# A recurrence feeding a gated FFN on one core: shorter weight conversion, the diagonal term on TensorE, smaller loads, a first batch in three units, scores copied whole

## The chip, the cores and the metric

The kernel runs on one core of one Trainium2 chip. The metric is the device time of one execution in microseconds (us); smaller is better. The engines of the core are TensorE (PE, with PEld for its weight loads), VectorE (DVE), ScalarE (ACT), GpSimd (POOL) and SyncE (SP), which here issues every transfer. Each engine has its own queue and takes its instructions in order.

## The reference

A recurrence over time in 4 batches, 8 heads, 768 tokens, head dimension 48, and an FFN on its result:

```python
for t in range(S):
    cur = np.einsum('bhd,bhe->bhde', u[None] * k[:, :, t], v[:, :, t])
    y[:, :, t] = np.einsum('bhd,bhde->bhe', r[:, :, t], state + cur)
    state = w[None, :, :, None] * state + np.einsum('bhd,bhe->bhde', k[:, :, t], v[:, :, t])
x = y.transpose(0, 2, 1, 3).reshape(B, S, H * D)           # 4 x 768 x 384
h = np.maximum(x @ w_in, 0.0)                              # 384 -> 1024
conv[t] = conv_w[0] * h[t-1] + conv_w[1] * h[t] + conv_w[2] * h[t+1]
out = (h * sigmoid(conv)) @ w_out                          # 1024 -> 384
```

The three FFN weights arrive as float64; the rest is float32.

## The kernel before

**The recurrence** is computed in chunks of 64 tokens; two chunks make a group of 128 tokens, six groups a batch, 24 groups in all. Heads go in pairs, A on partitions 64 to 111 and B on 0 to 47. For a group g:

- `load(g)` brings k and r with the head dimension on partitions (KR, 448 KB), k and r with tokens on partitions (KRT, 384 KB) and v (WW, 384 KB, half of it zeros).
- `prep(g)` scales KR by powers of the decay (TKR), copies the scaled r into the images RA and RB, makes the products of r, k and u on KRT and sums them over the head dimension (L450, into QQ): this is the diagonal term, a token's own r·u·k. POOL writes QQ into the diagonal of the score rows of RA and RB (affine_select, L462) and scaled k goes into KTA and KTB.
- `scores(g)` multiplies k and r on PE into psC (L477, L478), and DVE copies what lies under the mask into RA and RB (copy_predicated, L481, 64 partitions each).
- `step(g, c)` makes, for each chunk, the new state on PE (L493, L494, "S" below), which ACT copies from psS back to WW, and the chunk's outputs (L507, L508, "av" below) into psY.
- `yout(g)` copies psY to YY, moves the last head pair into place by six small transfers, and splits the result into a high part and a low part in XT.

**The FFN** works on units of about half a batch, each in 8 blocks of 128 hidden features. `first(i)` makes 9 products (L569) into one of two PSUM tiles HP, then relu, the middle tap, two more taps (CV, L577), sigmoid, the gate product SG (L581) and the split into GH and GL. `second(i)`, three blocks later, makes 9 products into PO (L598). Each matrix product of the FFN is made of three, so as to keep float32 accuracy: high by high, high by low, low by high.

**Weights** come in 17 pieces through `convert`: one of ACT and three of DVE (L398, L400, L402) make float32 out of the float64 bit pattern, ACT makes the high part and DVE or POOL subtracts for the low part.

**Order.** All this is first recorded as operations with durations and data keys; a list scheduler (`Plan`) puts them in one fixed order for each engine, by its own costs and by the offsets in `OFF`. Operations marked "any" go to DVE or POOL, whichever the planner thinks is free (their line is that of the helper `tt`, L288; transfers have that of `dma`, L291). The planner also places products with zeros (L653) where PE would rest. The program asks for as many thirds of groups (`pieces`) as the next FFN unit needs: `need(0)` is 4 groups for the first unit of 382 tokens.

Of the kernel before, what the change touches and what calls it, by code (L numbers as in the profile page):

```python
# [27 lines left out]
OFF = {  # microseconds by which classes of operations come earlier  # L28
# [26 lines left out]
U = 386                 # most tokens of a unit of the FFN  # L55
PAT = {"2": [(0, 382), (382, 386)], "s": [(0, 384), (384, 384)]}  # units of a batch: first token, tokens
UNITS = [(b,) + x for b in range(B) for x in PAT[UP[b]]]
NU = len(UNITS)
WS = 256.0              # the weights on chip are scaled by this


class Plan:
    """Operations in a valid order, with the resources they take and the data they read and write. They are
    issued in the order of a list schedule: each engine takes, of what can start, what the tensor engine's
    sequence needs first."""
# [3 lines left out]
    def __init__(self):  # L69
        self.ops = []  # L70
        self.last_w, self.last_r = {}, {}

    def op(self, eng, dur, rd, wr, fn, cls="", x=0.0):
# [19 lines left out]
        self.ops.append((dur, x, sorted(pred), fn, cls))  # L93
        return n
# [18 lines left out]
    def order(self):  # L113
# [22 lines left out]
        while todo:  # L136
# [30 lines left out]
            if e == "pe":  # L167
                # zero products where the engine would rest and its clock with it
# [19 lines left out]
                if att and cls not in ATT:  # L188
                    free[e] += 0.065
# [8 lines left out]
                # the part of the block before the end of the tick  # L198
# [13 lines left out]
            elif e == "sp":  # L212
                free[e] = s + d + 0.04
                dq = max(dq, s + d + 0.65) + x
# [3 lines left out]
            else:  # L218
                free[e] = s + d
# [17 lines left out]
LAT, LPE = 0.15, 0.21  # L237
ATT = ("th", "sc", "S", "av")


def rwkv_ffn_kernel(tc, krd, krt, vt, wd, ut, w_in, conv_w, w_out, out):
# [4 lines left out]
    with ExitStack() as ctx:  # L246
# [14 lines left out]
        KRT = sb([128, 2, NP, 2, D], F32, "KRT", NBUF)  # L261
# [22 lines left out]
        def tt(eng, n, rd, wr, cls="", **kw):  # L284
# [3 lines left out]
            op(eng, d, rd, wr, lambda e: e.tensor_tensor(**kw), cls)  # L288
# [18 lines left out]
        dma([], ["wc"], wc, wd)  # L307

# [14 lines left out]
        dma([], ["uu"], uu, ut)  # L323
# [3 lines left out]
        for o in (0, 64):  # L327
# [16 lines left out]
        # powers of the decay: PW[j] = w^j, TK = w^(31-j), TR = w^(j-32), DN = w^(95-j)  # L344
# [19 lines left out]
        op("dve", 0.53, ["PW"], ["PW2"], powers2)  # L364
        op("act", 0.32, ["PW", "PW2"], ["DN"], lambda e: A.copy(DN, PW[:, :, 95:31:-1]))
# [22 lines left out]
        ncv = [0]  # L388

        def convert(src, n, dst, view, keys):  # L390
# [5 lines left out]
            op("act", act(n), [("ST", i)], [("CC", i)],  # L396
               lambda e: A.activation(cc, s2[:, :, 1].bitcast(F32), AF.Copy, scale=2.0 ** -111))
            op("dve", dve(n, 1.6), [("ST", i)], [("TT", i)], lambda e: V.tensor_scalar(  # L398
                out=t, in0=s2[:, :, 1], scalar1=-2 ** 31, scalar2=None, op0=ALU.bitwise_and))
            op("dve", dve(n), [("CC", i)], [("TT", i)], lambda e: V.scalar_tensor_tensor(  # L400
                out=t, in0=cc.bitcast(I32), scalar=3, in1=t, op0=ALU.logical_shift_left, op1=ALU.bitwise_or))
            op("dve", dve(n), [("ST", i)], [("TT", i)], lambda e: V.scalar_tensor_tensor(  # L402
                out=t, in0=s2[:, :, 0], scalar=29, in1=t, op0=ALU.logical_shift_right, op1=ALU.bitwise_or))
# [19 lines left out]
        def prep(g):  # L423
            i = g % NBUF
            k_t, r_t = KRT[i][:, 0], KRT[i][:, 1]
# [16 lines left out]
            if g < DR:
                for o, T, nm in ((64, RA, "a"), (0, RB, "b")):
                    tt("dve", 512, ["TR1", "TR2", ("KR", i)], [("Rr", i, nm)] + ([("Rz", i)] if o == 0 else []),
                       out=v2(T[i], o, o + 48), in0=v2(RR[i], o, o + 48), in1=c2(TR[o:o + 48], 48), op=ALU.mult)
            else:
                for o, T, nm in ((64, RA, "a"), (0, RB, "b")):
                    dma([("KR", i)], [("Rr", i, nm)] + ([("Rz", i)] if o == 0 else []), T[i][o:o + 48], RR[i][o:o + 48], 0.625, 0.27, "rmv")
            tt("any", 384, [], [("KRT", i)], cls="p", out=r_t, in0=r_t, in1=k_t, op=ALU.mult)
            op("dve", dve(384), [("KRT", i)], [("QQ", i)], lambda e: V.tensor_reduce(  # L450
                out=QQ[i], in_=r_t.rearrange("q p c d -> q (p c) d"), op=ALU.add, axis=AX.X))
# [16 lines left out]
        def scores(g):  # L468
            i = g % NBUF
            ra, rb = (RA[i], RB[i]) if g < DR else (RR[i], RR[i])  # L470

            def mm(e):
                for c in range(2):
                    for p in range(NP):
                        t = slice(c * C, (c + 1) * C)
                        n = (2 * p + c) * C
                        PE.matmul(psC[0:64, n:n + C], KK[i][64:112, p, t], ra[64:112, p, t], start=True, stop=True)  # L477
                        PE.matmul(psC[64:128, n:n + C], KK[i][0:48, p, t], rb[0:48, p, t], start=True, stop=True)  # L478
            op("pe", 1.263, [("KR", i)] + ([("Rr", i, "a"), ("Rr", i, "b")] if g < DR else []), ["psAs", "psBs"], mm, "sc", 768)
            for o, T, ps, nm in ((0, RA, psC, "a"), (64, RB, psC, "b")):  # L480
                op("dve", 0.62, ["psAs" if o == 0 else "psBs", "mask"], [("Rs", i, nm)], lambda e, o=o, T=T, ps=ps: V.copy_predicated(  # L481
# [4 lines left out]
        def step(g, c):  # L486
            i = g % NBUF
            b, gi = divmod(g, GPB)
            if not (gi == GPB - 1 and c == 1):
                def smm(e):  # L490
                    for p in range(NP):
# [4 lines left out]
                op("pe", 0.495, [("KTk", i, "a"), ("KTk", i, "b"), ("KTd", i, "a", c), ("KTd", i, "b", c), ("KTd", i), ("Wv", i),  # L496
                                ("WS", i, c)], ["psAu", "psBu"], smm, "S", 720)
# [11 lines left out]
            op("pe", 0.6, [("Wv", i), ("WS", i, c), ("Rr", i, "a"), ("Rr", i, "b"), ("Rs", i, "a"), ("Rs", i, "b"), ("Rz", i)],  # L509
# [43 lines left out]
        def first(i):  # L553
# [18 lines left out]
            op("pe", 9 * (n + 8) / 2400.0, [("wi", 0, f), ("wi", 1, f), ("X", b % 2, 0), ("X", b % 2, S + 1)] + xs, [H_], mm, "f1", 9 * n)  # L572
# [15 lines left out]
        def second(i):  # L588
# [4 lines left out]
            for m in range(NM):  # L593
# [6 lines left out]
                op("pe", 3 * (n + 8) / 2400.0, [("wo", 0, f), ("wo", 1, f), ("GH", gi), ("GL", gi)], [f"o{m}"], mm, "f2", 3 * n)  # L600
# [116 lines left out]
```

## Time and profile before

| what | value |
|---|---|
| runs | 344.4, 344.5, 347.0 us (median 344.5) |
| span of the profiled execution | 343.2 us |
| busy PE, PEld, DVE, ACT, POOL | 311.8, 285.1, 270.4, 206.5, 193.7 us |
| first product of the FFN starts | 50.5 us |
| bytes read, written | 36.3 MB, 4.7 MB |
| mean granted clock of PE, 0 to 50.5, 50.5 to 124.5, then | 0.80, 0.91, 1.00 |

A busy share is an average over the span, and stages differ. An engine's busy time in a stretch says what holds that stretch; the idle time in front of an instruction, with what ended it, says what was late. A product's recorded length holds its way through the array, so the rate of PE is read from the distance of starts, not from lengths.

### The profile page before, as it was taken

The page shows a single profiled execution, that of the slowest core. Times are in us where ns is not written, and L with a number is a line of the kernel's source. Part 1 is how long each engine was busy: PE and PEld are TensorE (multiplying, and loading weights), DVE is VectorE, ACT ScalarE, POOL GpSimd, SP SyncE. Part 2 cuts the span into 40 slices and gives each one's busy share as a digit, 9 for nine tenths or more (in the row PEclk, how much of TensorE's full clock was granted, in tenths as well). Part 3 has the DMA queues.
Part 4 walks back from the last instruction along what each step waited for, and adds up shares of the span by engine and source line. Part 5 has one row for each costly group of instructions (what it writes and reads, how often), then busy time and mean ns, then how long its engine had stood idle before and what let it go on. Part 6 is the DMA issues. An engine that isn't in the chain of part 4 may idle for free.

```text
span 343.2 us, 8886 instructions
## 1 busy us (share of the span) xinstructions
PE 311.8 (91%) x3487; PEld 285.1 (83%) x3487; DVE 270.4 (79%) x409; ACT 206.5 (60%) x468; POOL 193.7 (56%) x200
## 2 busy tenths in 40 slices
PE   8698694997779988999998999899999999999996
PEld 4486474896668988899997999898999999999995
DVE  6899989989999999978778786786775756565550
ACT  4343446584765765567575663685566755876752
POOL 5998998697899988727455463333231212243230
PEclk9768969698998999999999999999999999999999
DMA  7996975977864297365566571544530200200101
GB/s 192 328 261 166 289 216 173 304 181 218 262 196 124 55 313 214 97 201 165 149 181 174 147 217 50 145 141 135 157 96 13 72 1 2 77 5 1 71 0 70
DMA packets 23882, 50.25 MB, mean 146 GB/s; under 512 B 4448, under 2 KB 10848, under 8 KB 23840
## 3 DMA queue, kind: packets, MB, share of 16 engines
q1 hardware_dynamic: 23840, 49.69, 50.0%
q8 instruction: 27, 0.44, 0.6%
q14 instruction: 15, 0.12, 0.1%
HBM read 36.30 MB, written 4.72 MB: 120 GB/s over the span
## 4 chain that ended last, share of the span: by engine, by line
PE 53%; DVE 17%; POOL 8%; issue 7%; DMA 7%; ACT 6%; SPq 1%; DVEq 0%; POOLq 0%; ACTq 0%
PE HP L569 20%; PE PO L598 19%; DMA KR<-in_krd_dram 4%; PE psC L477 4%; PE psY L507 3%; DVE CV L577 3%; PE psS L493 3%; POOL KRT L288 2%; DVE KR L288 2%; ACT SG L580 2%; DVE RB L481 2%; POOL RA L462 1%; DVE KRT L288 1%; DVE RA L481 1%; PE PO L653 1%
## 5 line engine op out<-in xcount | busy, mean ns | idle before, releaser
L569 PE MATMUL HP<-XT,wi 128*128 128x386 f32 (+2 forms) x576 | 116.1, 347 | 5.0 <-DVE SG L581 5.0
L598 PE MATMUL PO<-GH,wo 128*128 128x384 f32 (+2 forms) x384 | 111.6, 345 | 4.1 <-POOL wo L288 3.3
L569 PEld LDWEIGHTS HP<-XT,wi 128*128 128x128 f32 x576 | 103.4, 192 | 8.5 <-DVE SG L581 4.9
L288 POOL TENSOR_TENSOR GL<-SG,GH 128x384 fp32r<-128x384 f32 (+2 forms) x50 | 53.5, 1070 | 97.5 <-ACT GH L583 87.1
L577 DVE SCALAR_TENSOR_TENSOR CV<-HP,cw,CV 128x384 f32<-128x384 f32 (+2 forms) x128 | 78.2, 614 | 25.4 <-ACT CV L574 23.5
L598 PEld LDWEIGHTS PO<-GH,wo 128*128 128x128 f32 x384 | 71.0, 189 | 6.5 <-POOL wo L288 3.9
L598 PE MATMUL PO<-GL,wo 128*128 128x384 f32 (+2 forms) x192 | 65.3, 340 | 0.0
L580 ACT ACTIVATE SG<-CV 128x384 f32<-128x384 f32 (+2 forms) x64 | 33.5, 524 | 45.8 <-DVE CV L577 45.4
L581 DVE TENSOR_TENSOR SG<-HP,SG 128x384 f32<-128x384 f32 (+2 forms) x64 | 35.5, 555 | 21.1 <-ACT SG L580 20.4
L573 ACT ACTIVATE HP<-HP 128x386 f32<-128x386 f32 (+2 forms) x64 | 30.5, 477 | 23.2 <-PE HP L569 22.5
L583 ACT CAST GH<-SG 128x384 fp32r<-128x384 f32 (+2 forms) x64 | 32.8, 512 | 13.7 <-DVE SG L581 13.7
L500 ACT COPY WW<-psS 48x192 f32<-48x192 f32 x88 | 27.3, 311 | 20.3 <-PE psS L494 15.6
L288 DVE TENSOR_TENSOR KR<-KR,TKR 112x1024 f32<-112x1024 f32 (+1 forms) x24 | 36.2, 1509 | 3.9 <-DMA KR<-in_krd_dram 3.9
L574 ACT ACTIVATE CV<-HP,cw 128x384 f32<-128x384 f32 (+2 forms) x64 | 37.1, 579 | 1.3
L493 PEld LDWEIGHTS psS<-WW,KTA 112*48 112x48 f32 x352 | 21.6, 136 | 18.5 <-ACT WW L500 9.4
L493 PE MATMUL psS<-WW,KTA 112*48 112x48 f32 x352 | 27.2, 224 | 10.3 <-ACT WW L500 7.3
L598 PEld LDWEIGHTS PO<-GL,wo 128*128 128x128 f32 x192 | 36.5, 190 | 0.0
L507 PE MATMUL psY<-RA,WW 112*48 112x64 f32 x384 | 32.9, 233 | 0.9 <-ACT WW L500 0.9
L508 PE MATMUL psY<-RB,WW 128*48 128x64 f32 x384 | 32.4, 233 | 0.3 <-DVE RB L481 0.3
L477 PE MATMUL psC<-KR 48*64 48x64 f32 x352 | 26.2, 227 | 5.0 <-DVE RB L481 3.8
L507 PEld LDWEIGHTS psY<-RA,WW 112*48 112x48 f32 x384 | 26.5, 133 | 4.0 <-issue 2.2
L477 PEld LDWEIGHTS psC<-KR 48*64 48x64 f32 x352 | 23.1, 140 | 7.2 <-DVE RB L481 4.0
(80 smaller groups left out, 505.4 us busy)
## 6 DMA issues: line engine op xcount, KB each, us to landing
KR<-in_krd_dram SPq DMA_DIRECT2D x24, 448.0 KB, 4.6
KRT<-in_krt_dram SPq DMA_DIRECT2D x24, 384.0 KB, 5.5
WW<-in_vt_dram SPq DMA_DIRECT2D x24, 384.0 KB, 5.0
out_dram<-OS SPq DMA_DIRECT2D x18, 192.0 KB, 2.0
ST<-in_w_in_dram SPq DMA_DIRECT2D x8, 384.0 KB, 5.8
ST<-in_w_out_dram SPq DMA_DIRECT2D x8, 384.0 KB, 4.5
RA<-KR SPq DMA_DIRECT2D x22, 96.0 KB, 4.5
RB<-KR SPq DMA_DIRECT2D x22, 96.0 KB, 4.1
```

Source lines behind the costliest of these rows:

```text
L288: op(eng, d, rd, wr, lambda e: e.tensor_tensor(**kw), cls)
L477: PE.matmul(psC[0:64, n:n + C], KK[i][64:112, p, t], ra[64:112, p, t], start=True, stop=True)
L493: PE.matmul(psS[64:112, n:n + D], KTA[i][:, p, c, :], WA[i][:, p, c, :], start=True, stop=True)
L507: PE.matmul(psY[64:112, n:n + C], WA[i][:, p, c, :], RA[i][0:112, p, t], start=True, stop=True)
L508: PE.matmul(psY[0:48, n:n + C], WB[i][:, p, c, :], RB[i][:, p, t], start=True, stop=True)
L569: PE.matmul(hp, wi[a][:, j, fs], X[:, x, j, t], start=(j == 0 and k == 0), stop=(j == 2 and k == 2))
L574: op("act", act(n) + 0.05, [H_, "cw"], [("T", ti)], lambda e: A.activation(t1, hp[:, 1:n + 1], AF.Copy, scale=cw[:, 3 * f + 1:3 * f + 2]), ...
L577: op("dve", dve(n + 60), [H_, "cw"], [("T", ti)], lambda e, k=k: V.scalar_tensor_tensor(out=t1, in0=hp[:, k:n + k], scalar=cw[:, 3 * f + k ...
L580: op("act", act(n), [("T", ti)], [("SG", ti)], lambda e: A.activation(sg, t1, AF.Sigmoid))
L581: op("dve", dve(n), [H_], [("SG", ti)], lambda e: V.tensor_tensor(out=sg, in0=hp[:, 1:n + 1], in1=sg, op=ALU.mult), "GG")
L583: op("act", act(n), [("SG", ti)], [("GH", gi)], lambda e: A.copy(gh, sg))
L598: PE.matmul(PO[m][:, :n], wo[a][:, f, ms], g2[x], start=(f == 0 and k == 0), stop=(f == NF - 1 and k == 2))
```

## The change

It does these things:

- `convert`: ACT's scaling becomes a Prelu whose slope for negative values carries the sign, so that the step at L402 goes; the remaining pair of DVE operations is one shift and one shift-and-or.
- The diagonal term: KP = KK·RR for a group (112x512, on DVE or POOL), then 16 products on PE of 64 rows by one column with u·w (`uw`) as the moving operand, into columns 192 to 199 of psS ("q" below), and a copy to QQ on ACT. The products on KRT and the reduction go.
- `scores`, from the third group on: a 128x512 image SC holds the diagonal (eye·QQ, on DVE or POOL), one copy_predicated of 128 partitions writes the masked scores over it, and two transfers of 128 KB move its halves into RA and RB. The two affine_selects on POOL stay in groups 0 and 1 alone.
- Loads: of KRT only k (KT, 192 KB), of WW only the two blocks that aren't zero (two of 96 KB); the zero rows are written by POOL, at the start and, for the state, at each batch's start. RA and RB of groups 0 and 1 are copied by ACT rather than multiplied by DVE.
- The first batch is 3 units of 254, 256 and 258 tokens, so 72 blocks in all and not 64, and `need(0)` is 2 groups.
- The planner's costs of S, av, scores, products, a switch between recurrence and FFN (`SWITCH`), a transfer, and of DVE beside POOL change, and with them the whole order.

The core of the diff:

```diff
-UP = '2sss'
+UP = '3sss'
-PAT = {"2": [(0, 382), (382, 386)], "s": [(0, 384), (384, 384)]}
+PAT = {"2": ..., "s": ..., "3": [(0, 254), (254, 256), (510, 258)]}
-LAT, LPE = 0.15, 0.21
-ATT = ("th", "sc", "S", "av")
+LAT, LPE = 0.18, 0.21
+SLOWER, SHARED, SWITCH, XFER = 0.8, 1.25, 0.19, 1.45
+ATT = ("th", "sc", "S", "av", "q")
...
-            dma([], [("KRT", i)], KRT[i], krt[g], 0.45, 1.1, "ldT")
-            dma([], [("Wv", i), ("WS", i, 0), ("WS", i, 1)], WW[i], vt[g], 0.45, 1.1, "ldV")
+            dma([], [("KT", i)], KT[i], krt[g, :, 0], 0.45, 0.55, "ldT")
+            dma([], [("Wv", i, "a")], WA[i][0:64], vt[g, 0:64, 0], 0.45, 0.27, "ldV")
+            dma([], [("Wv", i, "b")], WB[i][64:128], vt[g, 64:128, 1], 0.45, 0.27, "ldV")
...
-               lambda e: A.activation(cc, s2[:, :, 1].bitcast(F32), AF.Copy, scale=2.0 ** -111))
-            op("dve", dve(n, 1.6), [("ST", i)], [("TT", i)], lambda e: V.tensor_scalar(
-                out=t, in0=s2[:, :, 1], scalar1=-2 ** 31, scalar2=None, op0=ALU.bitwise_and))
+            op("act", act(n), [("ST", i)], [("CC", i)], lambda e: A.activation(
+                cc, s2[:, :, 1].bitcast(F32), AF.Prelu, scale=2.0 ** -111, alpha=2.0 ** 32))
+            op("dve", dve(n, 2), [("ST", i)], [("TT", i)], lambda e: V.tensor_scalar(
+                out=t, in0=s2[:, :, 0], scalar1=29, scalar2=None, op0=ALU.logical_shift_right), port=True)
-            op("dve", dve(n), [("ST", i)], [("TT", i)], lambda e: V.scalar_tensor_tensor(
-                out=t, in0=s2[:, :, 0], scalar=29, in1=t, op0=ALU.logical_shift_right, op1=ALU.bitwise_or))
...
-            tt("any", 384, [], [("KRT", i)], cls="p", out=r_t, in0=r_t, in1=k_t, op=ALU.mult)
-            op("dve", dve(384), [("KRT", i)], [("QQ", i)], lambda e: V.tensor_reduce(
-                out=QQ[i], in_=r_t.rearrange("q p c d -> q (p c) d"), op=ALU.add, axis=AX.X))
+            tt("any", 512, [("KK", i), ("RR", i)], [("KP", g % 2)], out=kp, in0=KK[i], in1=RR[i], op=ALU.mult)
+            def qmm(e):
+                for p in range(NP):
+                    for c in range(2):
+                        n, t = NP * D + 2 * p + c, slice(c * C, (c + 1) * C)
+                        PE.matmul(psS[0:64, n:n + 1], kp[64:112, p, t], uw[64:112, p:p + 1], start=True, stop=True)
+                        PE.matmul(psS[64:128, n:n + 1], kp[0:48, p, t], uw[0:48, p:p + 1], start=True, stop=True)
+            op("act", 0.2, ["psAu", "psBu"], [("QQ", i)], lambda e: A.copy(QQ[i], psS[:, NP * D:NP * D + 2 * NP]))
...
+            if g >= DS:
+                sc = SC[g % 2].rearrange("q (a t) -> q a t", t=C)
+                op("dve", 0.68, ["psAs", "psBs", "mask"], [("SC", g % 2)], lambda e: V.copy_predicated(
+                    out=sc, mask=mask.unsqueeze(1).broadcast_to([128, NP * 2, C]), data=psC.rearrange("q (a t) -> q a t", t=C)), "Rs")
+                for o, T, nm in ((0, RA, "a"), (64, RB, "b")):
+                    dma([("SC", g % 2)], [("Rs", i, nm)], T[i][o:o + 64].rearrange("q p t -> q (p t)"), SC[g % 2][o:o + 64], 0.5, 0.36, "smv")
+                return
```

How the order changes is seen at three places. DVE at the first block of the FFN (CC, TT and ST are the buffers of the weight conversion, CV the gate's taps). Before:

```order
L400 SCALAR_TENSOR_TENSOR TT_115<-CC_112,TT_115 128x384
L398 TENSOR_SCALAR TT_116<-ST_110 128x384
L402 SCALAR_TENSOR_TENSOR TT_115<-ST_109,TT_115 128x384
L400 SCALAR_TENSOR_TENSOR TT_116<-CC_113,TT_116 128x384
L481 COPY_PREDICATED RA_61<-mask,psC 64x512
L402 SCALAR_TENSOR_TENSOR TT_116<-ST_110,TT_116 128x384
L481 COPY_PREDICATED RB_64<-mask,psC 64x512
L577 SCALAR_TENSOR_TENSOR CV_89<-HP_120,cw,CV_89 128x382
```

After, at the same place:

```order
L518 COPY_PREDICATED SC_135<-mask,psC 128x512
L424 SCALAR_TENSOR_TENSOR TT_116<-CC_113,TT_116 128x384
L422 TENSOR_SCALAR TT_118<-ST_112 128x384
L424 SCALAR_TENSOR_TENSOR TT_118<-CC_115,TT_118 128x384
L298 TENSOR_TENSOR XT_89<-YY_87,XT_89 128x3x128
L298 TENSOR_TENSOR wi_141<-TT_116,wi_140 128x3x128
L298 TENSOR_TENSOR KR_69<-KR_69,TKR 112x1024
L298 TENSOR_TENSOR KP_83<-KR_69 112x512
L620 SCALAR_TENSOR_TENSOR CV_91<-HP_122,cw,CV_91 128x254
```

A piece of weights has two rows on DVE where it had three, and a group's scores one where they had two; the first CV is DVE's row 47 where it was row 75.

SP's queue (all transfers) after the first groups; RA and RB are the images that the outputs read, YY the small moves of finished outputs. Before:

```order
L291 DMA RA_61<-KR_67 48x512
L291 DMA RB_64<-KR_67 48x512
L291 DMA YY_86<-YY_86 16x256 x2
L291 DMA WW_78<-in_vt_dram 128x768
L291 DMA YY_86<-YY_86 16x256
L291 DMA KTA_70<-KRT_79 64x384
L291 DMA KTB_73<-KRT_79 64x384
L291 DMA KR_67<-in_krd_dram 112x1024
```

After:

```order
L301 DMA KR_68<-in_krd_dram 112x1024
L301 DMA KTB_75<-KT_81 64x384
L301 DMA WW_78<-in_vt_dram 64x384 x2
L301 DMA YY_87<-YY_87 16x256 x2
L301 DMA RA_62<-SC_135 64x512
L301 DMA RB_65<-SC_135 64x512
L301 DMA YY_87<-YY_87 16x256 x4
L301 DMA RA_63<-SC_134 64x512
L301 DMA RB_66<-SC_134 64x512
L301 DMA KTA_70<-KT_79 64x384
```

Two transfers of scores for each group stand between the others, and v comes in two; in all SP issues 334 transfers where it issued 265.

PE in the first unit of the FFN, between two blocks' second products. Before:

```order
L598 MATMUL PO_124<-GH_97,wo_136 128x382
L598 MATMUL PO_124<-GL_102,wo_136 128x382
L598 MATMUL PO_124<-GH_97,wo_137 128x382
L569 MATMUL HP_120<-XT_87,wi_134 128x384 x2
L569 MATMUL HP_120<-XT_87,wi_135 128x384
```

After:

```order
L641 MATMUL PO_126<-GH_98,wo_142 128x254
L641 MATMUL PO_126<-GL_103,wo_142 128x254
L641 MATMUL PO_126<-GH_98,wo_143 128x254
L612 MATMUL HP_122<-XT_89,wi_140 128x256 x2
L612 MATMUL HP_122<-XT_89,wi_141 128x256
```

In the first batch the same nine products run over 256 to 260 columns (second ones 254 to 258), in 24 blocks where there were 16. In PE's order five groups' scores and six S stand ahead of the FFN's first product, where seven and eleven did; the FFN gives way to the recurrence 52 times where it did 24 times.

More of the change, by code (lines that the diff above doesn't have):

```diff
@@ L16 @@
 DK = 8
+DS = 2
 LAG = 3
@@ L218, in order @@
             else:
+                if e == "dve" and self.port[i]:
+                    d += SLOWER * max(0.0, min(d, free["pool"] - s))
+                if e == "pool" and free["dve"] > s:
+                    d *= SHARED
                 free[e] = s + d
@@ L260, in rwkv_ffn_kernel @@
         WA, WB = [x[0:112, 0] for x in WW], [x[:, 1] for x in WW]
-        KRT = sb([128, 2, NP, 2, D], F32, "KRT", NBUF)
+        KT = sb([128, NP, 2, D], F32, "KT", NBUF)
+        KP = sb([112, NP, GT], F32, "KP", 2)
         QQ = sb([128, NP * 2], F32, "QQ", NBUF)
@@ L307, in rwkv_ffn_kernel @@
         dma([], ["wc"], wc, wd)
+        for o, q in ((0, 64), (64, 0)):
+            dma([], [("uc", o)], uc[o:o + 48], ut[q].rearrange("p d -> d p"))
         def warm(e):
@@ L333, in rwkv_ffn_kernel @@
                 compare_op=ALU.is_gt, fill=0, base=0, channel_multiplier=-1))
+        op("pool", 0.1, [], ["eye"], lambda e: G.memset(eye, 1.0))
+        for o in (0, 64):
+            op("pool", 0.2, [], ["eye"], lambda e, o=o: G.affine_select(
+                out=eye[o:o + 64], in_=eye[o:o + 64], pattern=[[1, C]],
+                compare_op=ALU.is_equal, fill=0.0, base=0, channel_multiplier=-1))
         op("dve", 0.6, [], ["psY"], lambda e: V.memset(psY, 0.0))
@@ L364, in rwkv_ffn_kernel @@
         op("dve", 0.53, ["PW"], ["PW2"], powers2)
+        for o in (0, 64):
+            op("dve", 0.1, ["wc", ("uc", o)], [("uw", o)], lambda e, o=o: V.tensor_tensor(
+                out=uw[o:o + 48], in0=uc[o:o + 48], in1=wc[o:o + 48], op=ALU.mult))
         op("act", 0.32, ["PW", "PW2"], ["DN"], lambda e: A.copy(DN, PW[:, :, 95:31:-1]))
@@ L424, in prep @@
             i = g % NBUF
-            k_t, r_t = KRT[i][:, 0], KRT[i][:, 1]
+            k_t = KT[i]
             def c2(ap, n):
@@ L442, in prep @@
[L442 to L448, printed above, removed]
@@ L449, in prep @@
-            tt("any", 384, [], [("KRT", i)], cls="p", out=r_t, in0=r_t, in1=k_t, op=ALU.mult)
-            op("dve", dve(384), [("KRT", i)], [("QQ", i)], lambda e: V.tensor_reduce(
-                out=QQ[i], in_=r_t.rearrange("q p c d -> q (p c) d"), op=ALU.add, axis=AX.X))
+                tt("dve", 1024, ["TK1", "TK2", "TR1", "TR2"], [("KK", i), ("RR", i)], "KR", out=kr, in0=kr, in1=TKR.rearrange(
+                    "q a p t -> q (a p) t").unsqueeze(2).broadcast_to([112, 2 * NP, 2, C]), op=ALU.mult)
+            else:
+                for T, W, ks, key in ((KK, TK, ["TK1", "TK2"], "KK"), (RR, TR, ["TR1", "TR2"], "RR")):
+                    tt("dve", 512, ks, [(key, i)], "KR", out=v2(T[i], 0, 112), in0=v2(T[i], 0, 112), in1=c2(W, 112), op=ALU.mult)
@@ new lines, in prep @@
+            for o, T, nm in ((64, RA, "a"), (0, RB, "b")):
+                wr = [("Rr", i, nm)] + ([("Rz", i)] if o == 0 else [])
+                if g < DR:
+                    op("act", act(512), [("RR", i)], wr, lambda e, o=o, T=T: A.copy(T[i][o:o + 48], RR[i][o:o + 48]), "Rr")
+                else:
+                    dma([("RR", i)], wr, T[i][o:o + 48], RR[i][o:o + 48], 0.625, 0.27, "rmv")
+            kp = KP[g % 2]
+            tt("any", 512, [("KK", i), ("RR", i)], [("KP", g % 2)], out=kp, in0=KK[i], in1=RR[i], op=ALU.mult)
@@ L456, in prep @@
             else:
-                tt("any", 384, ["TH0", "TH1"], [("KRT", i)], out=k_t, in0=k_t,
+                tt("any", 384, ["TH0", "TH1"], [("KT", i)], out=k_t, in0=k_t,
                    in1=TH.unsqueeze(2).broadcast_to([128, NP, 2, D]), op=ALU.mult)
                 for o, T, nm in ((0, KTA, "a"), (64, KTB, "b")):
-                    dma([("KRT", i)], [("KTk", i, nm)], T[i][o:o + 64], k_t[o:o + 64], 0.625, 0.27, "kmv")
+                    dma([("KT", i)], [("KTk", i, nm)], T[i][o:o + 64], k_t[o:o + 64], 0.625, 0.27, "kmv")
@@ new lines, in prep @@
+            if g % GPB == 0:
+                for o, T in ((64, WA), (0, WB)):
+                    op("pool", 0.35, [("Wz", i)], [("WS", i, 0)], lambda e, o=o, T=T: G.memset(T[i][o:o + 48, :, 0, :], 0.0), "WS0")
+            if g >= DS:
+                sc = SC[g % 2].rearrange("q (a t) -> q a t", t=C)
+                tt("any", 512, [("QQ", i), "eye"], [("SC", g % 2)], "dg", out=sc, in0=eye.unsqueeze(1).broadcast_to([128, NP * 2, C]),
+                   in1=QQ[i].unsqueeze(2).broadcast_to([128, NP * 2, C]), op=ALU.mult)
+                return
```

55 lines of the change are left out of this document (28 added, 27 removed).

## The prediction

> **What bounds the kernel now.** I read the page's head and its slices first, then busy time by stage, then the vector engine's groups in the first stage, then the pitch of the products on TensorE in a stretch that nothing interrupts. The page and its chain:
>
> ```profile
> span 343.2 us, 8886 instructions
> PE 311.8 (91%) x3487; PEld 285.1 (83%) x3487; DVE 270.4 (79%) x409; ACT 206.5 (60%) x468; POOL 193.7 (56%) x200
> PE   8698694997779988999998999899999999999996
> DVE  6899989989999999978778786786775756565550
> PE 53%; DVE 17%; POOL 8%; issue 7%; DMA 7%; ACT 6%; SPq 1%; DVEq 0%; POOLq 0%; ACTq 0%
> ```
>
> The page alone says "TensorE at 91%". The slices (8.6 us each) say that two regimes lie behind it: up to about slice 16 DVE stands at 9 and PE has gaps; from slice 18 PE stands at 9 and DVE falls to 5. Busy time by stage (columns: stretch, length, PE, PEld, DVE, ACT, POOL, granted clock), then the gate products SG (L581) alone, of which each FFN block has one, and the start and length of the twelfth in the timeline:
>
> ```profile
> 0.00:50.50 50.50, 40.30 (x622) 29.67 (x622) 45.27 (x67) 21.06 (x57) 43.08 (x55) 0.80 0.84 239
> 50.50:124.50 74.00, 61.40 (x743) 54.33 (x740) 71.75 (x104) 48.19 (x109) 65.10 (x58) 0.91 0.69 199
> 124.50:343.20 218.70, 210.11 (x2128) 201.15 (x2126) 153.41 (x240) 137.24 (x305) 85.53 (x89) 1.00 0.37 107
> 0.00:124.50 124.50, 6.59 (x12) 0.86 0.75 215
> ...
> 123.89 0.56 DVE L581 TENSOR_TENSOR SG<-HP,SG 128x386 f32<-128x386 f32 x1
> ```
>
> In the first 124.5 us DVE is busy for 117.0 us and idle for 7.5, with PE at 101.7 us (part of that at a clock below 1). The gate product of FFN block 12, at 123.9 us, ends that stretch, and by then every weight is converted. Behind it PE is busy for 210.1 of 218.7 us at clock 1.00. So the time is roughly DVE's list of work up to block 12, then PE's list of work from there. I forecast both.
>
> **The first stage: DVE's list.** DVE's groups in 0 to 124.5 us (count, busy us and mean ns):
>
> ```profile
> L288 DVE TENSOR_TENSOR KR<-KR,TKR 112x1024 f32<-112x1024 f32 (+1 forms) x13 | 20.1, 1547 | 1.7 <-DMA KR<-in_krd_dram 1.7
> L577 DVE SCALAR_TENSOR_TENSOR CV<-HP,cw,CV 128x382 f32<-128x382 f32 (+1 forms) x24 | 14.5, 606 | 0.1
> L402 DVE SCALAR_TENSOR_TENSOR TT<-ST,TT 128x384 int32<-128x384 int32 (+1 forms) x17 | 13.4, 794 | 0.1
> L481 DVE COPY_PREDICATED RB<-mask,psC 64x512 f32<-64x512 int32 x12 | 8.9, 741 | 0.4
> L481 DVE COPY_PREDICATED RA<-mask,psC 64x512 f32<-64x512 int32 x12 | 8.7, 727 | 1.5 <-POOL RB L462 1.2
> L450 DVE TENSOR_REDUCE QQ<-KRT 128x8 f32<-128x384 f32 x13 | 7.0, 542 | 1.0 <-POOL KRT L288 0.9
> L581 DVE TENSOR_TENSOR SG<-HP,SG 128x382 f32<-128x382 f32 (+1 forms) x12 | 6.6, 549 | 0.6 <-ACT SG L580 0.5
> L288 DVE TENSOR_TENSOR KRT<-KRT,TH 128x384 f32<-128x384 f32 x4 | 4.2, 1048 | 0.0
> L288 DVE TENSOR_TENSOR RB<-KR,TKR 48x512 f32<-48x512 f32 x2 | 2.1, 1036 | 0.0
> L288 DVE TENSOR_TENSOR XT<-YY,XT 128x384 fp32r<-128x384 f32 x2 | 1.9, 934 | 0.0
> L288 DVE TENSOR_TENSOR RA<-KR,TKR 48x512 f32<-48x512 f32 x2 | 1.8, 914 | 0.0
> L288 DVE TENSOR_TENSOR KTB<-KRT,TH 64x384 f32<-64x384 f32 x2 | 1.4, 724 | 0.1
> L288 DVE TENSOR_TENSOR wi<-TT,wi 128x384 fp32r<-128x384 f32 x2 | 1.4, 716 | 0.0
> L288 DVE TENSOR_TENSOR KRT<-KRT,uu 128x384 f32<-128x384 f32 x2 | 1.1, 548 | 0.0
> ```
>
> Counted in the two orders up to block 12's gate product, at these means:
>
> - Copies of scores, 23 to 11: one 128x512 copy takes the place of two of 64x512, and more partitions do not lengthen a row, so 0.74 each: -8.8.
> - The third conversion step (L402) goes, 17 times: -13.5. The sign comes with ACT's scaling, whose form stays one activation.
> - The reduction goes, 13 times: -7.1. Products with u and r·k on KRT, 4 on DVE: -2.75.
> - KR products of 1024, 11 to 8, because fewer groups are prepared by block 12: -4.9. TH products, 4 to 1: -2.65. RA and RB products of groups 0 and 1 move to ACT: -3.9. One XT subtraction fewer: -0.9.
> - 24 CV at 254 or 256 columns for 382 or 386, about 0.475 for 0.606: -3.2. 12 SG likewise: -1.6.
> - Added: two KR products of 512, +1.8; two KTA/KTB, +1.6; two low parts of weights, +1.6; one GL and uw, +0.7; four KP at 112x512 and three diagonal images at 128x512. No row has these two. The nearest, wi at 0.716 for 384 columns, gives 0.93 for 512: +3.7 and +2.8. Bounds: 0.7 (the 548 ns row scaled) and 1.4 (the 1048 ns row scaled), so -1.6 to +3.3 on the sum.
>
> The sum is -37.1, so block 12's gate product stands at 123.9 - 37.1 = 86.8 us. POOL covers the rest: at before's means its list up to there is about 69 us (11 GL at 0.77, six KP at 1.8, four diagonal images at 1.8, 13 low parts of weights and outputs at 1.2, 19 other products at 1.2, fills), so it does not take DVE's place. Nor does ACT: 24 more QQ copies at 0.2 each and four more 512-column copies make 7 us against 29 us that it idles in the first 50.5 of before and 26 in the next 74.
>
> **The second stage: PE's list.** The chain of waits late in the run, then the start times of an attention burst (start, us):
>
> ```profile
> 255.45 1.59 PE HP L569 x9
> 260.01 1.77 PE PO L598 x9
> 308.22 1.59 PE PO L598 x9
> 309.81 1.59 PE HP L569 x9
> 330.42 9.44 PE PO L598 x54
> ```
>
> ```profile
> 256.97 0.24 PE L493 MATMUL psS<-WW,KTA 112*48 112x48 f32 x1
> 257.37 0.22 PE L507 MATMUL psY<-RA,WW 112*48 112x64 f32 x1
> 257.92 0.27 PE L477 MATMUL psC<-KR 48*64 48x64 f32 x1
> 259.00 0.24 PE L493 MATMUL psS<-WW,KTA 112*48 112x48 f32 x1
> 259.39 0.22 PE L507 MATMUL psY<-RA,WW 112*48 112x64 f32 x1
> 259.94 0.44 PE L598 MATMUL PO<-GH,wo 128*128 128x384 f32 x1
> ```
>
> Nine products of 384 to 388 columns take 1.59, a pitch of 0.177; 384 columns at 0.16 plus some 0.016 a product. For 254 to 260 columns I scale the columns and keep the 0.016: 0.1225, so 1.10 a set of nine. No row shows a product of that length; bounds 0.117 (wholly proportional) and 0.177 (no shorter than now). A step's state products (S) take 0.395, its outputs (av) 0.55, a group's scores 1.08. The first set behind a burst takes 0.2 more (1.77 for 1.59). The diagonal's 16 products of one column (32 passes) have no row: nearest are the state products, 32 passes in 0.395, and with a psS change of hands 0.55; bounds 0.4 and 1.08.
>
> The change order leaves behind block 13's first products: 11 short first sets (12.1), 48 long (76.3), 47 short thirds of second sets at 0.37 (17.3), 144 long at 0.525 (75.6), 15 scores (16.2), 32 S (12.6), 35 av (19.3), 15 diagonals (8.3) and 38 bursts at 0.2 (7.6): 245.3. Block 13 starts about when block 12 is through, since the two HP tiles gate it. 86.8 + 245.3 + 3.4 (from the last product's end, 330.42 + 9.44, to the span's end) = 335.5. For waits I add 3.4: before, the same sum from block 16 on came out 5.5 us short of its span, and the new stage has fewer groups left to wait for. That gives 338.9 in span. The runs' median, 344.5, stands 1.3 above the profiled execution's span, so 340.2; I say 340.
>
> The change also makes PE's list longer: 24 short blocks cost 24 x 2.2 = 52.8 for 16 x 3.17 = 50.7; diagonals 24 x 0.55 = 13.2; 52 turns from FFN to attention for 24, +5.6. Together PE gains 21 us of work while DVE loses 37 ahead of block 12. That is why -37 becomes -4.
>
> **Moves that I cost at nothing.** Scores now go copy, two transfers, then use. Issues and landings in before:
>
> ```profile
> L291 SPq DMA_DIRECT2D RA<-KR x22: 509/541/1494, 20.6 to 252.0; - x22
> L291 SPq DMA_DIRECT2D RB<-KR x22: 503/582/728, 22.4 to 252.6; - x22
> RA<-KR SPq DMA_DIRECT2D x22, 96.0 KB, 4.5
> ```
>
> 0.75 + 1.1 + 4.5 = 6.3 us from scores to outputs, where the new order puts 9.3 to 21.9 us of PE work between them. If PE ran that stretch in less, or the queue held the pair by 3 us, PE would stop there, up to 22 times. SP's queue is in order: the transfers wait for the copy, and the YY moves and KR loads behind them wait too. By block 12 SP has about 110 issues; at 0.55 that is 60 of 87 us. The Trainium skill, "SBUF — State Buffer", § "Can I just issue two DMAs to hit both halves?", speaks against moving scores and V in halves of 64 partitions: it says that two transfers on the two halves run one after the other, 6% better than one alone. By that a pair lands one transfer later, about 9 us by my estimate from the 4.5 us row, and the shortest distance (9.3) would just be missed; that belongs to rival C and changes no term here. No row tests it, since the RA and RB moves above are issued half a microsecond apart.
>
> **Rivals.**
>
> A, larger gain. DVE is no longer what PE waits for even before block 12, because the contended means (wi 716 beside POOL, KRT 548 alone) fall with POOL's list 40 us shorter. Then only PE's own list counts: some 36 us up to the first FFN block (50.5 before, where seven scores and eleven S stand ahead of it; five and six now), 287 behind it, 3.4 of tail, and some 2 to 4 of waits: 328 to 331. For it: DVE's groups still hold about 13 us of contention. Against: the early groups need DMA, DVE, PE and ACT in a chain, and the same sum for before (50.5, 261 of products, 3.4) leaves 28 us of waits.
>
> B, slower. Short products do not get cheaper with their columns. The weight load behind each is:
>
> ```profile
> L569 PEld LDWEIGHTS HP<-XT,wi 128*128 128x128 f32 x576 | 103.4, 192 | 8.5 <-DVE SG L581 4.9
> ```
>
> Its mean is 192 ns, longer than the present pitch of 177, so it runs side by side with products and may itself set a floor. At a pitch of 0.177 the 240 short products behind block 12 cost 13 us more: 353. The rival is slower than the median once the pitch is over about 0.142. Against: a load's record may contain its wait for the products ahead. The Trainium skill, "TensorE: Matmul & The Clock Gate", § LDWEIGHTS, gives a load as its columns divided by 1.2, about 107 ns for 128 columns; by that floor the sum stays at 340. The 192 of the row neither agrees nor refutes, since nothing here shows a load that has no product to wait for.
>
> C, about the same. SP's queue or the scores' trip ends last in places: 196 issues by the end of the first batch's share, at 0.55, is 108 us; a stop of 0.3 us in most of 22 groups costs 5 to 8: 345 to 348.
>
> D, the change does less on DVE: KP and the diagonal images at 1.4 and long waits at the start of each burst, block 12 at 92: 344 to 346. It falls under "same", with C.
>
> **How the numbers follow.** The forecast (334 to 341.1) has 0.40, A 0.17, C with D 0.24, B 0.19. About 1% is what a measurement of this kernel can tell from no change: 341.1 to 348.0. Forecast and A make "faster" 0.54 (a small part of the forecast lies at its upper edge), C and D and that edge make "same" 0.26, B 0.20. The range 329 to 352 takes in most of A, all of C, D and the lower half of B.
>
> **What would show it.** DVE through block 12's gate product at 84 to 90 us; no L402 or reduction; a whole-score copy near 0.74; KP and diagonal near 0.93; short first sets of 1.05 to 1.15; diagonals at 0.4 to 0.7; PE at 9 from slice 11 on; 240 to 250 us from block 13 to the last product. Wrong would be: short sets over 1.28 (B), PE waiting at L550 for the RA and RB transfers or SP idle never (C), or block 12 under 80 us (A) or over 92 (D).

## The result and the profile after

The changed kernel takes 356.5 us (median; 355.4 to 357.0) where the kernel before took 345.0 in the same runs: 1.033 times as long, interval 1.029 to 1.037. The forecast was 340, with 329 to 352 as its range. Times in this text are medians; one execution of a later run, e5, took 1576.9 us, which nothing here explains, and is left out of e5's median. The changed kernel's head, slices and chain:

```profile
span 354.6 us, 10924 instructions
PE 338.8 (96%) x4439; PEld 311.8 (88%) x4439; DVE 239.6 (68%) x387; ACT 215.4 (61%) x531; POOL 150.4 (42%) x159
PE   7899898859999999999999999999999999999996
DVE  7969969898676777776765666566534665565560
PE 85%; DVE 8%; DMA 3%; issue 2%; ACT 2%; SPq 0%; DVEq 0%
```

The change did what it says: DVE has 30.8 us less to do, POOL 43.3 less. But TensorE has 27.0 us more, its slices stand at 9 from the tenth on, and the chain that ends last is TensorE's for 85% where it was 53%. TensorE's idle time fell from 31.4 to 15.8 us; 27.0 more of work against 15.6 less of waiting is the 11.4 us.

Busy time by stage (stretch, length, PE, PEld, DVE, ACT, POOL, granted clock), and the gate product of block 12 in the timeline:

```profile
0.00:38.90 38.90, 34.07 (x606) 26.23 (x606) 33.34 (x47) 20.22 (x54) 32.35 (x48) 0.96 0.74 198
38.90:80.00 41.10, 33.49 (x473) 29.71 (x473) 36.05 (x59) 28.42 (x72) 26.26 (x27) 0.86 0.74 211
80.00:98.00 18.00, 18.00 (x260) 16.86 (x262) 13.68 (x24) 9.36 (x27) 11.44 (x9) 0.84 0.56 143
98.00:354.60 256.60, 253.26 (x3110) 239.00 (x3104) 156.58 (x260) 157.37 (x380) 80.31 (x76) 1.00 0.39 108
...
97.42 0.43 DVE L624 TENSOR_TENSOR SG<-HP,SG 128x256 f32<-128x256 f32 x1 [1.59 <-ACT SG L623]
```

Block 12 comes at 97.4 us, 26.5 earlier than before, but 10.6 later than forecast. From 80 us on TensorE is busy all the time but for the last 3 us, so it took over from DVE at 80 us and not behind block 12. What is left behind block 12 takes 257.2 us, where the forecast had 252.1 (245.3, tail and waits). 10.6 and 5.1 are the whole miss of 15.7 in span.

The new operations on DVE up to 98 us, and one burst of the diagonal's products in the timeline, its first rows and its last:

```profile
L298 DVE TENSOR_TENSOR KP<-KR 112x512 f32<-112x512 f32 x4 | 4.2, 1051 | 0.0
L518 DVE COPY_PREDICATED SC<-mask,psC 128x512 f32<-128x512 int32 x7 | 5.2, 738 | 1.6 <-PE psC L514 1.6
L298 DVE TENSOR_TENSOR SC<-eye,QQ 128x512 f32<-128x512 f32 x3 | 3.0, 989 | 0.0
```

```profile
201.19 0.21 PE L476 MATMUL psS<-uw,KP 48*64 48x1 f32 x1
201.20 0.21 PE L477 MATMUL psS<-uw,KP 48*64 48x1 f32 x1
201.27 0.19 PE L476 MATMUL psS<-uw,KP 48*64 48x1 f32 x1
...
202.09 0.19 PE L476 MATMUL psS<-uw,KP 48*64 48x1 f32 x1
```

The copies and images cost about what they should, KP somewhat more (1.05 for 0.93). The diagonal's burst starts at 201.19 and its last pair at 202.09, with 0.058 between pairs: 1.03 us up to the next product, the pace of the scores (1.08 for 16 products with 64 moving columns), although one column moves. The forecast had 0.55.

The short sets came out as forecast. From the chain of waits:

```profile
98.88 1.09 PE HP L612 x9
99.96 0.36 PE PO L641 x3
```

### The profile page after: what moved, and what is told of

It reads as the page before. It is cut to its first block, busy times and chain, and to the rows that moved or that the text cites. A ratio compares the mean times of both kernels' runs of the same rounds, so it can differ in the third digit from the quotient of the medians.

```text
span 354.6 us, 10924 instructions
## 1 busy us (share of the span) xinstructions
PE 338.8 (96%) x4439; PEld 311.8 (88%) x4439; DVE 239.6 (68%) x387; ACT 215.4 (61%) x531; POOL 150.4 (42%) x159
## 4 chain that ended last, share of the span: by engine, by line
PE 85%; DVE 8%; DMA 3%; issue 2%; ACT 2%; SPq 0%; DVEq 0%
PE PO L641 30%; PE HP L612 29%; PE psY L550 6%; PE psC L513 5%; PE psS L476 5%; PE psS L536 5%; PE PO L696 2%; DVE KR L298 2%; DMA KR<-in_krd_dram 2%; DVE TT L422 2%; DVE TT L424 1%; DMA RB<-SC 1%; PE psS L477 1%; PE psY L551 1%; PE psS L537 1%
## 5 line engine op out<-in xcount | busy, mean ns | idle before, releaser
L612 PE MATMUL HP<-XT,wi 128*128 128x386 f32 (+3 forms) x648 | 118.3, 328 | 4.2 <-DVE SG L624 3.6
L641 PE MATMUL PO<-GH,wo 128*128 128x384 f32 (+3 forms) x432 | 119.7, 333 | 0.6 <-ACT wo L430 0.5
L620 DVE SCALAR_TENSOR_TENSOR CV<-HP,cw,CV 128x384 f32<-128x384 f32 (+3 forms) x144 | 81.7, 569 | 31.5 <-ACT CV L617 29.8
L298 POOL TENSOR_TENSOR GL<-SG,GH 128x384 fp32r<-128x384 f32 (+3 forms) x46 | 49.2, 1069 | 116.4 <-ACT GH L626 95.0
L641 PE MATMUL PO<-GL,wo 128*128 128x384 f32 (+3 forms) x216 | 69.7, 322 | 0.0
L616 ACT ACTIVATE HP<-HP 128x386 f32<-128x386 f32 (+3 forms) x72 | 31.8, 441 | 38.4 <-PE HP L612 37.3
L624 DVE TENSOR_TENSOR SG<-HP,SG 128x384 f32<-128x384 f32 (+3 forms) x72 | 36.6, 509 | 26.9 <-ACT SG L623 26.2
L623 ACT ACTIVATE SG<-CV 128x384 f32<-128x384 f32 (+3 forms) x72 | 35.1, 488 | 29.2 <-DVE CV L620 28.9
L617 ACT ACTIVATE CV<-HP,cw 128x384 f32<-128x384 f32 (+3 forms) x72 | 39.3, 546 | 1.2
L626 ACT CAST GH<-SG 128x384 fp32r<-128x384 f32 (+3 forms) x72 | 34.1, 474 | 6.9 <-DVE SG L624 6.8
```

What stands on the lines that cost most here:

```text
L298: op(eng, d, rd, wr, lambda e: e.tensor_tensor(**kw), cls, port=True)
L612: PE.matmul(hp, wi[a][:, j, fs], X[:, x, j, t], start=(j == 0 and k == 0), stop=(j == 2 and k == 2))
L617: op("act", act(n) + 0.05, [H_, "cw"], [("T", ti)], lambda e: A.activation(t1, hp[:, 1:n + 1], AF.Copy, scale=cw[:, 3 * f + 1:3 * f + 2]), ...
L620: op("dve", dve(n + 60), [H_, "cw"], [("T", ti)], lambda e, k=k: V.scalar_tensor_tensor(out=t1, in0=hp[:, k:n + k], scalar=cw[:, 3 * f + k ...
L623: op("act", act(n), [("T", ti)], [("SG", ti)], lambda e: A.activation(sg, t1, AF.Sigmoid))
L624: op("dve", dve(n), [H_], [("SG", ti)], lambda e: V.tensor_tensor(out=sg, in0=hp[:, 1:n + 1], in1=sg, op=ALU.mult), "GG")
```

## The experiments

All times are medians beside runs of the kernel before on the same chip, about 345 us. Two theories stood at the start. P: TensorE's own list is the bound from 80 us on, and the diagonal's products are its under-priced term. R: the new order's waits and turns set the time, and the diagonal lies in their shadow.

**e1, the diagonal's products cut to two of 16, same order.**

```diff
-                for p in range(NP):
-                    for c in range(2):
+                for p in range(NP if g < 2 else 1):
+                    for c in range(2 if g < 2 else 1):
```

> The changed kernel with the diagonal's products cut from 16 to 2 in groups 2 to 23 (the diagonal then uses old numbers for most columns; everything else, the order too, is as it was). Theory P, that TensorE's list is the bound from 80 us on and that the diagonal's products are its under-priced term (1.02 us a group in the trace, 0.55 in the prediction): 14 of 16 products are 0.89 us a group, 16 groups of them behind 80 us, so 14 to 20 us less, 336 to 343 us. Theory R, that the new order's waits and turns between recurrence and FFN set the time and the diagonal lies in their shadow: within 4 us of 356.

339.9 us, ratio to before 0.988 (0.984 to 0.992). Of TensorE's busy time 19.4 us went and of the span 17.0. A burst of two products takes 0.21 us at full clock. P holds, R falls.

**e2, each of the diagonal's products made twice, same order.**

```diff
-                for p in range(NP):
+                for p in [x for x in range(NP) for _ in range(1 if g < 2 else 2)]:
```

> The changed kernel with each of the diagonal's products made twice in groups 2 to 23, same order, same result. P: 1.02 us more a group, at least the 16 groups behind 80 us, 372 to 380 us. R: 356 to 362 us, since a longer burst would still lie in the shadow of waits.

391.9 us, 1.136 (1.128 to 1.144): R falls again, and P's figure is too small. The bursts grew from 1.03 to 1.96, which is 20.5 us; the span grew by 35.6. The rest goes with a lower granted clock, 0.92 over the span for 0.97. Two stretches of the doubled kernel in which TensorE never rests, then the same length in the changed kernel:

```profile
90.00:120.00 30.00, 30.00 (x502) 28.30 (x504) 17.06 (x32) 15.61 (x45) 10.25 (x10) 0.89 0.48 127
150.00:250.00 100.00, 100.00 (x1415) 94.03 (x1415) 57.85 (x93) 52.22 (x128) 33.32 (x31) 0.93 0.51 136
```

```profile
90.00:120.00 30.00, 30.00 (x550) 27.75 (x550) 20.97 (x39) 18.25 (x54) 10.63 (x10) 1.00 0.53 145
150.00:250.00 100.00, 100.00 (x1391) 93.15 (x1390) 64.95 (x101) 60.24 (x145) 39.78 (x35) 1.00 0.55 147
```

The granted clock (the column behind POOL) is 0.89 and 0.93 for 1.00, at 100% busy in both. Where it falls points to the added products as the cause: between 90 and 306 us the clock falls to half in ten stretches of 3 to 7 us, for example to 0.52 from 210.0 to 213.5 us, and each of the ten begins within 2 us of the end of one of the 16 doubled bursts (that one ends at 210.0).

**e9, the diagonal as four products of 128 weight columns.** The two heads of a pair are told apart by zeros in `uw`, and four small ACT copies take the place of one.

```diff
-                for p in range(NP):
-                    for c in range(2):
-                        n, t = NP * D + 2 * p + c, slice(c * C, (c + 1) * C)
-                        PE.matmul(psS[0:64, n:n + 1], kp[64:112, p, t], uw[64:112, p:p + 1], start=True, stop=True)
-                        PE.matmul(psS[64:128, n:n + 1], kp[0:48, p, t], uw[0:48, p:p + 1], start=True, stop=True)
+                for p in range(NP):
+                    n = NP * D + 2 * p
+                    PE.matmul(psS[:, n:n + 2], kp[:, p, :], uw[:, p, :], start=True, stop=True)
```

> The changed kernel with the diagonal's 16 products (64 weight columns, one moving column) made as four (128 weight columns, two moving columns, the two heads of a pair told apart by zeros in uw) and four small ACT copies in place of one; the planner makes a new order. If the price goes by the number of products: 0.2 to 0.4 us a group where it was 1.03, 16 groups behind 80 us, 343 to 349 us. If it goes by the weight columns loaded (512 a group, where pairs of 64 ran side by side): 0.8 to 1.0 us a group, 353 to 358 us.

355.5 us, 1.026 (1.016 to 1.035). Two bursts in its timeline, the first at full clock, the second at half, each with the row that follows:

```profile
190.45 0.95 PE L476 MATMUL psS<-uw,KP 112*128 112x2 f32 x8
191.33 0.26 PE L556 MATMUL psY<-RA,WW 112*48 112x64 f32 x1
```

```profile
14.10 1.71 PE L476 MATMUL psS<-uw,KP 112*128 112x2 f32 x8
15.66 0.37 PE L702 MATMUL PO<-wz 128*128 128x256 bf16 x1
```

The four products are eight passes (a float32 product is two rows of the trace). They take 0.88 us up to the next instruction, and 1.56 where the granted clock was 0.50. So a quarter of the products costs nearly the same: the price goes by the weight columns loaded, 110 ns for 128 of them at full clock, and not by the number of products; nor by the moving columns, as far as the scores' 64 beside the diagonal's one show. The Trainium skill, "TensorE: Matmul & The Clock Gate", § LDWEIGHTS, has a load take its columns divided by 1.2 in ns, 107 ns for 128 by estimate. This run agrees at full clock with its 110; at half the clock it has 195.

**e4, the diagonal term back on DVE, the rest of the change kept.** r is loaded with its tokens on partitions again; two products on DVE or POOL and a reduction on DVE make QQ; KP, `uw` and the products on TensorE go.

```diff
-            tt("any", 512, [("KK", i), ("RR", i)], [("KP", g % 2)], out=kp, in0=KK[i], in1=RR[i], op=ALU.mult)
-            op("pe", 0.4, [("KP", g % 2), ("uw", 0), ("uw", 64)], ["psAu", "psBu"], qmm, "q", 16)
+            tt("any", 384, ["uu"], [("RT", i)], "KRT", out=r_t, in0=r_t, in1=uu.unsqueeze(2).broadcast_to([128, NP, 2, D]),
+               op=ALU.mult)
+            tt("any", 384, [("KT", i)], [("RT", i)], "p", out=r_t, in0=r_t, in1=k_t, op=ALU.mult)
+            op("dve", dve(384), [("RT", i)], [("QQ", i)], lambda e: V.tensor_reduce(
+                out=QQ[i], in_=r_t.rearrange("q p c d -> q (p c) d"), op=ALU.add, axis=AX.X))
```

> The changed kernel with the diagonal term made as before (r loaded with tokens on partitions, two products on DVE or POOL, a reduction on DVE), and all else of the change kept; the planner makes a new order. P: TensorE loses 24.5 us of products, DVE gains 7 of reductions and about 5 of products ahead of block 12, so block 12 at about 102 us and 241 us behind it: 341 to 346 us. R: 353 us or more.

334.5 us, 0.972 (0.969 to 0.975): faster than both kernels, and by more than P's figure. Its page and stages:

```profile
PE 313.0 (94%) x3680; PEld 286.9 (86%) x3680; DVE 246.9 (74%) x411; ACT 213.8 (64%) x507; POOL 170.8 (51%) x181
```

```profile
80.00:98.00 18.00, 18.00 (x287) 16.90 (x286) 14.66 (x30) 12.09 (x34) 13.78 (x15) 1.00 0.93 230
98.00:333.90 235.90, 230.39 (x2548) 218.34 (x2546) 159.39 (x264) 152.77 (x353) 97.81 (x94) 1.00 0.47 128
```

DVE took the work back for 7.3 us over the whole span (246.9 for 239.6) and POOL for 20.4 (170.8 for 150.4), TensorE lost 25.8, and it runs at clock 1.00 between 80 and 98 us where the changed kernel had 0.84.

**e8, e4 with scores copied in two as before.** Edit: `DS = 2` becomes `DS = 99`.

> The changed kernel with the diagonal term made as before (334.5 us) and scores as before (two copies of 64 partitions onto RA and RB, POOL's two affine_selects), all else of the change kept. 22 copies of 0.74 us back on DVE and 44 affine_selects of 0.85 us back on POOL. If DVE's list ahead of block 12 still counts: 8 to 9 copies, 6 to 8 us more, 340 to 343 us. If TensorE's list alone counts from 80 us on: 334 to 337 us.

333.2 us, 0.969 (0.963 to 0.974). Its interval and e4's overlap: copying scores whole is worth nothing that these two runs can tell. This is the lowest median of all runs.

**e6, e4 with the first batch in two units.** Edit: `UP = '3sss'` becomes `UP = '2sss'`.

> The changed kernel with the diagonal term made as before (334.5 us) and with the first batch in two units as before. If three units help by starting the FFN on two groups rather than four: 8 to 12 us more, 342 to 347 us. If TensorE's list is all that counts: 24 x 2.2 against 16 x 3.17 us and fewer turns, 2 to 5 us less, 330 to 333 us.

338.6 us, 0.981 (0.977 to 0.984): three units are worth about 4 us, in the direction of the first expectation and half its size.

**e10, the kernel before with the diagonal on TensorE alone.** Edit: the products on KRT, the reduction and `uu` go; KP, `uw`, the 16 products (the planner is told 1.02) and ACT's copy to QQ come in.

> The kernel before with the diagonal term on TensorE alone (KP on DVE or POOL, 16 products, QQ copied by ACT; RA and RB filled as before), the planner told 1.02 us for it. P: TensorE's list grows by 24.5 us, about 12 groups of it behind block 12, DVE's falls by 7 us ahead of it: 350 to 358 us. If the diagonal's relief of DVE and POOL outweighs it: 336 to 343 us.

393.6 us, 1.136 (1.127 to 1.144): 48 us above the kernel before, where P said 5 to 13. The groups that wait on TensorE:

```profile
L463 PE MATMUL psS<-uw,KP 48*64 48x1 f32 x384 | 30.3, 205 | 11.7 <-ACT WW L515 10.5 <-DVE uw L368 0.9 <-POOL KP L289 0.3
L508 PE MATMUL psS<-WW,KTA 112*48 112x48 f32 x352 | 28.9, 236 | 11.3 <-ACT QQ L466 6.2 <-ACT WW L515 4.8
```

Diagonal and state products share psS, and in this order each waits for ACT to clear the other's result: 10.5 and 6.2 us, 16.7 together, where the changed kernel shows 0.5. The clock in its first 88 us was 0.63. So this run shows a second price of the move, not the size of the first; how much is the order's doing, and what the low clock cost, stays open.

**e13, the changed kernel with a lighter DVE, same order.** 16 of 17 combining steps of the conversion (L424) aren't issued, so the weights come out nearly zero.

> The changed kernel in its own order with 16 of the 17 combining steps of the weight conversion (L424) not issued; the weights are then nearly zero. DVE's list ahead of block 12 loses 16 x 0.738 = 11.8 us, TensorE's nothing. If DVE still sets when block 8 comes (79.4 us, with TensorE idle 6 us between 60 and 80): block 8 five to nine us earlier and the end as much, 348 to 352 us. If TensorE's own list and its chain with ACT set it: block 12 within 2 us of 97.4, 354 to 357 us.

351.8 us, 1.021 (1.015 to 1.027); span 348.8. Block 8's gate product moved from 79.4 to 75.8 and block 12's from 97.4 to 91.7. Of the 11.8 us taken off DVE 4.7 reached the end by the medians, 5.8 by the spans. But the clock was higher too. The changed kernel from 40 to 100 us, then this one:

```profile
40.00:60.00 20.00, 18.57 (x283) 16.71 (x283) 16.37 (x31) 15.72 (x38) 11.60 (x13) 0.91 0.69 196
60.00:80.00 20.00, 13.82 (x190) 11.90 (x186) 18.58 (x28) 12.70 (x35) 13.56 (x12) 0.81 0.77 216
80.00:100.00 20.00, 20.00 (x278) 18.78 (x279) 15.68 (x27) 11.13 (x31) 11.87 (x10) 0.85 0.55 139
```

```profile
40.00:60.00 20.00, 18.73 (x299) 16.98 (x299) 14.91 (x28) 15.93 (x39) 13.60 (x16) 1.00 0.77 227
60.00:80.00 20.00, 15.62 (x221) 13.84 (x219) 13.73 (x26) 14.45 (x40) 15.55 (x15) 0.91 0.82 239
80.00:100.00 20.00, 20.00 (x348) 18.59 (x344) 15.86 (x28) 12.68 (x36) 11.28 (x10) 1.00 0.58 156
```

Two executions with the same mean clock, 0.976, took 353.3 us here and 355.4 in the changed kernel. So DVE's list still counts ahead of block 8, but 2 us are left at the same clock, and whether the lighter list or the zero weights raised the clock stays open.

**e3, e5 and e12, the shorter conversion alone.** e3 lets the planner make a new order. In e5 and e12, the same kernel twice, every engine keeps its old order and L402 isn't issued.

```diff
-                out=t, in0=s2[:, :, 1], scalar1=-2 ** 31, scalar2=None, op0=ALU.bitwise_and))
+                out=t, in0=s2[:, :, 0], scalar1=29, scalar2=None, op0=ALU.logical_shift_right))
...
-            op("dve", dve(n), [("ST", i)], [("TT", i)], lambda e: V.scalar_tensor_tensor(
-                out=t, in0=s2[:, :, 0], scalar=29, in1=t, op0=ALU.logical_shift_right, op1=ALU.bitwise_or))
```

> The kernel before with the shorter weight conversion alone. If DVE's list ahead of block 12 passes through to the end, as the prediction has it: 17 x 0.79 = 13.4 us earlier, 331 to 335 us. If another engine takes over at once: 339 to 345 us.

> The kernel before, every engine in its old order, with the shorter weight conversion: the 17 operations of L402 aren't issued and the other two are those of the change. If the prediction's step holds (DVE's list ahead of block 12 passes through): up to 17 x 0.79 = 13.4 us less, 331 to 337 us; then the 351 us of the same edit with a new order were that order's doing. If DVE did not set the time there: 342 to 346 us.

> The kernel before, in its old order, with the shorter conversion, once more, for its profile: 335 to 340 us again, and block 12's gate product 7 to 13 us ahead of 123.9.

e3: 351.2 us, 1.020 (1.015 to 1.025), slower than before and against both of its expectations. e5: 336.3, 0.978 (0.972 to 0.985); e12: 337.9, 0.981 (0.972 to 0.989). In e12 block 12's gate product comes at 115.1 us, 8.8 earlier than before, and the span ends 7.3 earlier (335.9 for 343.2). Stages of e3, then of e12:

```profile
0.00:60.00 60.00, 41.79 (x724) 30.84 (x724) 54.02 (x79) 24.57 (x64) 51.00 (x61) 0.91 0.83 241
60.00:125.00 65.00, 52.74 (x623) 48.75 (x621) 61.58 (x91) 43.58 (x96) 46.04 (x42) 0.92 0.70 209
```

```profile
0.00:60.00 60.00, 46.01 (x711) 35.47 (x712) 53.62 (x77) 28.59 (x72) 49.94 (x63) 0.86 0.87 248
60.00:125.00 65.00, 57.99 (x698) 51.48 (x696) 61.97 (x87) 45.32 (x104) 62.00 (x56) 1.00 0.81 222
```

In e3 the planner gave the freed DVE time to operations that either engine may take: DVE is as busy as in e12 (115.6 us of 125), POOL 14.9 us less, TensorE 9.5 us less. The same shortening is worth about -7 us in the old order and +7 in the new one. That the planner's choice between DVE and POOL is the reason is read from these stages alone; no run fixes it by itself.

**e7, the kernel before with the planner's new costs, and e11, e8 with measured costs.** e11's edit gives scores, S and av 1.08, 0.40 and 0.55 us for 0.5, 0.2 and 0.25.

> The kernel before with the planner's new costs alone: the same operations in a new order. If the order's quality is a term of its own: 3 to 10 us away from 344.5, to either side. If the order hardly matters while the list of work is the same: 343 to 346 us.

> The 333 us kernel (diagonal and scores as before, all else of the change kept) with the planner told the measured 1.08, 0.40 and 0.55 us of scores, S and av, where the change told it 0.5, 0.2 and 0.25. If the understated costs spoil the order: 2 to 6 us less, 327 to 331 us. If the order hardly depends on them: 331 to 336 us.

e7: 343.6 us, 0.996 (0.994 to 0.999), no difference to speak of. e11: 341.3 us, 0.989 (0.982 to 0.996), 7 slower than e8 by the two ratios: truer costs made a worse order, against both expectations.

## Why the prediction was wrong

The step that failed first is the price of the diagonal: "nearest are the state products, 32 passes in 0.395". The state products are 8, in 16 passes (352 rows each at L493 and L494 over 44 steps); the diagonal's 16 products are 32 passes, as many as the scores', and the 1.08 us of the scores stood there as the upper bound. The runs put it at 1.03, against 0.55. For the 15 groups behind block 12 that is 7 us, and the rest of the list behind it came out 2 us shorter than forecast. Over 24 groups 0.48 us is 11.5 us; e1 returned 17.0 us of span for 22 x 0.82 = 18.0 of products, so about 10 of the 15.7 us missed lie in this one term. The reason was at hand: the rule on loads that rival B cites from the Trainium skill, "TensorE: Matmul & The Clock Gate", § LDWEIGHTS, was held against the FFN's 128-column loads and not against the diagonal's 64-column ones.

The second is "DVE's list of work up to block 12, then PE's". DVE's list itself was sized well: 83.1 us busy to 98 us, against 79.9 forecast. But DVE idled 15 us there, not 7.5. Of these, 10.6 lie ahead of 80 us, mostly waits for the scores' products (4.1) and for ACT (3.6), and 4.3 behind it, where TensorE never rests. So TensorE became the bound four blocks earlier than forecast, and its list ahead of block 12 wasn't summed in the forecast. It held nine diagonals (4 us more than at the forecast price) and ran at clock 0.84 to 0.86 from 39 to 98 us. e1 moved block 12 by 4.8 us with DVE's work as it was, e13 by 5.7 with TensorE's as it was, and most of that stood at block 8 already (3.9 and 3.6). So both lists count in that stage; how much each counts stays open, since the clock differed in both runs. In the old order the step held in the main: of 13.4 us off DVE's list (e12) 8.8 reached block 12 and 7.3 the end, there too with a higher clock (1.00 for 0.90 from 60 to 125 us).

Two small terms of DVE's list don't follow from the trace of before: four products on KRT and three with TH are 2.6 and 3.1 us at their means, for 2.75 and 2.65. That changes nothing.

What held: short sets at 1.09 for 1.10; scores' copies at 0.74 and images at 0.99 for 0.93; no output product waited for the transfers of scores, although one of them stands in the chain that ended last, for 3.8 us at 33.6 us; other stops by the queue of SP (rival C) aren't seen. The larger gain (rival A) did not come, though its mechanism, TensorE's list as the bound ahead of block 12 as well, is what the trace shows from 80 us on. Rival B was right in its sign and wrong in its mechanism: short products did get cheaper with their columns, while products of one column did not. The rest of the change was sound, since e4 keeps all of it but the diagonal and wins 10 us. Moving that one term to the engine that bounds the rest of the run lost 17 us in the same order (e1) and 22 with a new one (e4).

## What to carry to other kernels

Price a product by its weight columns and passes as well as by its moving columns: here a product that moves one column costs what its load costs. Before moving work off a busy engine, sum the whole list of the engine that gets it, and ask from which point on that engine is the bound; here that was four blocks ahead of block 12. When a planner makes the order, test an edit in the old order too: the same shortening was worth about -7 and +7 us in two orders.

## What the runs showed of the hardware

Long bursts of products that move one column can lower TensorE's clock although the engine counts as busy: with bursts of 1.96 us the granted clock was 0.89 to 0.93 in stretches where TensorE was 100% busy, falling to half right behind bursts, and the kernel lost 35.6 us for 20.5 us of added products; with bursts of 1.03 us it stayed at 1.00 in the same stretches. Four products of 128 weight columns took 0.88 us and sixteen of 64, in pairs, 1.03. And the Prelu that carries the sign costs ACT nothing: 538 ns for 533 in the old order, ACT as busy as it was (205.7 us for 206.5), while DVE lost 10.5.
